# Sixteen hashed-attention heads and two feed-forward blocks on one core: the unit copies of the first two head pairs moved to ScalarE, a third raw buffer, and the product of two weights moved six steps ahead

## The chip, the cores and the metric

The kernel runs on one core of one Trainium2 chip. TensorE multiplies and transposes, ScalarE and VectorE read its results out of PSUM, GpSimd (POOL) and SyncE (SP) issue DMAs. The metric is the device time of one launch in microseconds (us), the median of several runs.

## What is computed

Attention whose mask is "same hash bucket", 2 batches of 8 heads with 768 positions of 64 numbers, then two feed-forward blocks on 1536 tokens of 512 numbers. All is fp32 to the caller; the weights arrive as fp64.

```python
q_bits = (einsum('bhsd,dk->bhsk', q, proj) > 0)       # 6 bits; the same for k
mask = q_bucket[:, :, :, None] == k_bucket[:, :, None, :]
scores = where(mask, scale * q @ k.T, -1e9)
attn = softmax(scores)                                 # row maximum taken off first
x = (attn @ v)  ->  (1536, 512)
h = x @ w_in; g = h * tanh(softplus(h)); x2 = g @ w_out          # d_ff 2048
a = x2 @ w1; b = x2 @ w2; out = ((a * b) @ w3) @ w_out2          # d_ff 1024
```

## The kernel before

**Attention in 96 steps.** A pair of heads is one p (8 pairs). A half of a pair's query rows is one j (16 of them), and a j has 6 steps, each a block of 128 query rows of one head: step n has j = n // 6. `scores` multiplies the block with all keys into a PSUM tile `ts` (two matmuls on `ka`/`qa`, which hold the bits too, two on `kb`/`qb`), `maxima` (VectorE) takes the row maxima, `expo` (ScalarE) takes the exponential into `E`. `unit` transposes three blocks of `E` on TensorE into PSUM (`et`), a copy brings them to SBUF (`etf`), and `av` multiplies them with v. There are 12 unit copies per j, two in each step; before, ScalarE makes 7 of the 12 and VectorE 5. `norm`, `rb_mm`, `rb_act` and `x_out` apply the row sums and store 192 KB of x.

**Preparing a pair.** For each head and each of q and k, `split_hi` (ScalarE) and `split_lo` (VectorE) cut fp32 into two parts, `qk_transpose` transposes them into PSUM (`tqk`), `qk_act` copies that out in two ScalarE activations (`qb`/`kb`, then `qa`/`ka`), `bits_mm` multiplies with the projection (`tb`) and `bits_dve` writes the bits (VectorE, 12x768). The first head is prepared ahead of step 0 (the prologue), the rest inside the steps.

**One ring of two PSUM tiles** (`ps_s`, tag "s") holds `ts`, `tqk`, `tb` and `w3p`. A tile can be written again only when its reader is through: `expo` for `ts`, `qk_act` for `tqk`, `bits_dve` for `tb`.

**Weights.** fp64 arrives as pairs of int32. `load64` (on POOL's queue) loads 1 MB into a raw buffer (2 of them), and three steps turn it into fp32: `decode_a` (ScalarE), `decode_b1` (two VectorE instructions), `decode_b2` (one). Since a*b is followed by two products with no function between, the kernel first computes wp = w3 @ w_out2 in the shadow of attention: w_out2 in four parts (`pre_a` to `pre_c`, `wo2_hi`, `wo2_lo`), w3 in eight blocks of 128 rows (`w3_trans` into `w3p`, `w3_hi`, `w3_lo`), and for each block f 24 matmuls of 512 columns into `wacc` (`wp_mm`), stored by `wp_out`. Later steps decode the first chunks of w_in and w_out (`chunk_dec` to `issue_lo`), split the first x (`x_load`, `x_hi`, `x_lo`) and begin the first feed-forward product (`h_early`, from step 83).

**The order.** `at(n, where, fn)` puts a piece of work at step n; the main loop runs the places of a step in a fixed order, and `pin` keeps every engine to it:

```python
run(n, "pr"); scores; run "la"; maxima; run "nm", "lv", "un", "av", "mm"; expo
then "pe" (transposes, bit products), "ea" (ScalarE), "ev" (VectorE), "dm" (DMAs)
```

So a bit product (`tb`) at a step's "pe" stands behind that step's `ts` and units, and the `bits_dve` of it at the next step's "lv" behind that step's maxima. `MM` says how many of a block's 24 matmuls stand in a step, by n % 6. After attention a list (`prog`) of products over three blocks of 512 tokens runs to the end; its order on each engine is the scheduler's.

Of the kernel before, what the change touches and what calls it, by code (L numbers as in the profile page):

```python
# [18 lines left out]
F32 = mybir.dt.float32  # L19
# [15 lines left out]
def kernel(  # L35
# [43 lines left out]
    def load64(src, n, pool=strm, queue=nc.sync):  # L79
        raw = pool.tile([128, n, 1024 // n, 2], I32, tag="raw", name="raw", bufs=2)  # L80
        queue.dma_start(out=raw.rearrange("p a b t -> p a (b t)"), in_=src)
        return raw, pool
# [393 lines left out]

    def qk_act(u, nm):
        t = spare_ps.pop((u, nm))
        f = [
            pf.tile([128, S], FR, tag=nm + h, name=nm + h, bufs=3) for h in "ab"  # L480
        ]
        feats[u, nm] = f
        scale = 1.0 if nm == "q" else 1.0 / float(D) ** 0.5
        nc.scalar.activation(
            out=f[1].rearrange("p (a n) -> p a n", a=2), in_=t[:, :, 0:HS].bitcast(F32),
            func=AF.Copy, scale=scale,
        )
# [113 lines left out]

    def unit(j, e, kt):
        t = ps.tile([128, 512], F32, tag="et", name="et", bufs=2)
        for ci in range(CH):
            nc.tensor.transpose(  # L605
                t[:, ci * 128:(ci + 1) * 128],
                E[j, e * CH + ci][:, kt * 128:(kt + 1) * 128],
                ident,
            )
        f = pa.tile([128, HS], F32, tag="etf", name="etf", bufs=NR)  # L610
        act = kt % 2 == 0 or (e == 0 and kt == 3)
        (nc.scalar.copy if act else nc.vector.tensor_copy)(out=f, in_=t[:, 0:HS])  # L612
        eth[j, e, kt] = f
# [44 lines left out]
    def pre_c(nm, i):  # L658
        pre[nm, i] = decode_b2(pre[nm, i])
        x = PRE.index((nm, i)) + 2  # L660
        if x < len(PRE):
            pre_load(x)
# [184 lines left out]
    for i, nm in enumerate("qk"):  # L847
# [18 lines left out]
    for n in range(max(NS + 6, HEND + 2)):  # L866
# [188 lines left out]
```

## Time and profile before

| what | value |
|---|---|
| median of 3 runs | 860.73 us (858.62 to 861.25) |
| the profiled execution | 859.71 us, span 857.9 us |
| PE busy | 811.0 us (95%) |
| DVE busy | 513.1 us (60%) |
| ACT busy | 455.7 us (53%) |
| chain that ended last | PE 76%, DVE 12%, ACT 5%, issue 3%, DMA 3% |

The span is the time between the first and the last instruction that the profiler saw; the profiled execution's own time is 1.8 us more. In the table of stretches below, PEclk is the clock that TensorE was granted (1.00 is 2.4 GHz, 0.50 is 1.2 GHz), and the boundaries of the stretches are starts of the maxima instruction (L551) of a step: 12.49 is step 0, 38.66 step 6, 111.23 step 24, 139.07 step 30, 280.36 step 66, 347.41 step 84.

### The profile page before, as it was taken

Reading aid. Unit: us, or ns where it says so; the run is one execution under the profiler, and the core shown is the slowest. Engines: PE = TensorE matmul, PEld = TensorE weight load, DVE = VectorE, ACT = ScalarE, POOL = GpSimd, SP = SyncE. Lnnn points to the kernel's source line nnn. Section 1 sums busy time; section 2 is a strip of 40 time slices with the busy share of each in tenths; the row PEclk is TensorE's granted clock in tenths of the full one; section 3 lists DMA queues with packets and bytes.
Section 4 is the critical chain, followed back from the end, with each engine's and each line's share of the span. In section 5 each row is a group of like instructions: output and inputs, shape, how many; then the busy total and the mean of one; then the engine's idle time right before and its main releaser. Section 6 shows DMA issues by size and latency. Waiting matters only on the chain.

```text
span 857.9 us, 10511 instructions
## 1 busy us (share of the span) xinstructions
PE 811.0 (95%) x4145; PEld 630.0 (73%) x4145; DVE 513.1 (60%) x711; ACT 455.7 (53%) x691; POOL 75.2 (9%) x131
## 2 busy tenths in 40 slices
PE   6678879999999998999999999999999999999998
PEld 4556657777777775677887888888888888888886
DVE  5577777777777788867997874333444343324422
ACT  5566756666667777776654643333343333333321
POOL 1000000000000000101231211000110110110000
PEclk8799989999999999999999999999999999999999
DMA  5112313232322324344887754242332234322101
GB/s 190 56 50 90 131 59 127 70 114 72 126 71 97 123 84 135 126 159 149 300 292 281 247 196 125 96 148 98 107 113 75 82 116 147 98 99 74 48 1 50
DMA packets 34593, 103.45 MB, mean 121 GB/s; under 512 B 3184, under 2 KB 11632, under 8 KB 33520
## 3 DMA queue, kind: packets, MB, share of 16 engines
q0 software_dynamic: 20928, 81.80, 27.9%
q1 hardware_dynamic: 13472, 20.85, 7.2%
q8 instruction: 33, 0.54, 0.3%
q14 instruction: 16, 0.13, 0.0%
q10 hardware_dynamic: 144, 0.13, 0.0%
HBM read 81.79 MB, written 20.97 MB: 120 GB/s over the span
## 4 chain that ended last, share of the span: by engine, by line
PE 76%; DVE 12%; ACT 5%; issue 3%; DMA 3%; POOL 0%; ACTq 0%; DVEq 0%; POOLq 0%
PE abp L944 16%; PE hps L334 12%; PE x2a L917 11%; PE oac L968 8%; PE ts L540 8%; PE pv L620 6%; PE et L605 4%; PE wacc L703 4%; DVE st L551 4%; PE tb L500 3%; DVE qa L509 2%; DMA raw<-in_moe_w_dram 2%; ACT E L562 2%; PE rb L587 2%; PE tqk L470 1%
## 5 line engine op out<-in xcount | busy, mean ns | idle before, releaser
L551 DVE TENSOR_REDUCE st<-ts 128x1 f32<-128x768 f32 x96 | 91.9, 957 | 93.5 <-PE ts L540 93.4
L944 PE MATMUL abp<-x2hl,hl 128*128 128x512 f32 x576 | 137.5, 395 | 0.0
L334 PE MATMUL hps<-xhl,hl 128*128 128x512 f32 x552 | 133.2, 395 | 0.8 <-ACT mh L361 0.8
L917 PE MATMUL x2a<-ghl,hl 128*128 128x512 f32 x552 | 132.0, 397 | 1.7 <-DVE ghl L379 1.7
L944 PEld LDWEIGHTS abp<-x2hl,hl 128*128 128x128 f32 x576 | 108.3, 188 | 25.6
L269 DVE TENSOR_TENSOR hl<-f,hl 128x1024 fp32r<-128x1024 f32 x60 | 73.4, 1224 | 89.7 <-ACT hl L264 89.7
L917 PEld LDWEIGHTS x2a<-ghl,hl 128*128 128x128 f32 x552 | 104.8, 190 | 26.6 <-DVE ghl L379 2.0
L334 PEld LDWEIGHTS hps<-xhl,hl 128*128 128x128 f32 x552 | 102.9, 188 | 26.3 <-issue 2.4
L562 ACT ACTIVATE E<-ts,st 128x768 f32<-128x768 f32 x96 | 95.5, 995 | 26.1 <-DVE st L554 25.7
L612 ACT COPY etf<-et 128x384 f32<-128x384 f32 x112 | 52.1, 480 | 61.4 <-PE et L605 61.1
L605 PE MATMUL et<-ident,E 128*128 128x128 f32 x576 | 82.3, 280 | 0.1
L264 ACT CAST hl<-f 128x1024 fp32r<-128x1024 f32 x60 | 62.8, 1046 | 26.2 <-PE abp L944 12.0
L605 PEld LDWEIGHTS et<-ident,E 128*128 128x128 f32 x576 | 71.1, 144 | 5.6 <-DVE etf L612 0.8
L620 PE MATMUL pv<-etf,rv 128*64 128x384 f32 x384 | 74.3, 510 | 0.0
L540 PE MATMUL ts<-ka,qa 76*128 76x384 f32 x192 | 56.1, 374 | 15.2 <-ACT E L562 9.2
L968 PE MATMUL oac<-hl,phl 128*128 128x512 f32 x288 | 69.8, 393 | 0.0
L968 PEld LDWEIGHTS oac<-hl,phl 128*128 128x128 f32 x288 | 54.2, 188 | 12.4
L953 DVE TENSOR_TENSOR asb<-abp,asb 128x512 f32<-128x512 f32 x24 | 16.6, 691 | 72.2 <-ACT asb L952 72.2
L952 ACT COPY asb<-abp 128x512 f32<-128x512 f32 x24 | 14.0, 585 | 85.0 <-PE abp L944 85.0
L703 PE MATMUL wacc<-wo,w3t 128*128 128x512 f32 x192 | 56.9, 418 | 0.0
L89 ACT ACTIVATE g<-raw 128x1024 f32<-128x1024 f32 x36 | 41.2, 1144 | 27.5 <-DMA raw<-in_moe_w_out_dram 10.4
L379 DVE TENSOR_TENSOR ghl<-mh,ghl 128x1024 fp32r<-128x1024 f32 x24 | 29.3, 1223 | 38.9 <-ACT ghl L378 38.9
(108 smaller groups left out, 967.9 us busy)
## 6 DMA issues: line engine op xcount, KB each, us to landing
raw<-in_moe_w_dram POOLq DMA_DIRECT2D x16, 1024.0 KB, 5.5
raw<-in_moe_w_out_dram POOLq DMA_DIRECT2D x12, 1024.0 KB, 8.1
raw<-in_moe_w_in_dram POOLq DMA_DIRECT2D x8, 1024.0 KB, 6.8
f<-keep_wi POOLq DMA_DIRECT2D x16, 512.0 KB, 3.6
f<-keep_wo POOLq DMA_DIRECT2D x16, 512.0 KB, 3.6
f<-wp_d POOLq DMA_DIRECT2D x12, 512.0 KB, 4.0
keep_wi<-g POOLq DMA_DIRECT2D x8, 512.0 KB, 4.8
keep_wo<-g POOLq DMA_DIRECT2D x8, 512.0 KB, 3.1
```

What stands on the lines that cost most here:

```text
L264: nc.scalar.copy(out=hl[:, 0], in_=f)
L269: nc.vector.tensor_sub(out=hl[:, 1], in0=f, in1=hl[:, 0])
L334: nc.tensor.matmul(o, lhsT=w[:, ws, kk, f * 128:(f + 1) * 128], rhs=xh[xs][:, kk, :], start=(m == 0), stop=(m == 3 * KD - 1),)
L540: nc.tensor.matmul(t[:, a, 0:HS], lhsT=l[0:kk, qt * 128:(qt + 1) * 128], rhs=r[0:kk, a * HS:(a + 1) * HS], start=(l is qa), stop=(l is qb),)
L551: nc.vector.tensor_reduce(out=s[:, i, 1:2], in_=sc[j, i][:, :, 0:HS], axis=AX.XY, op=ALU.max, negate=True)
L562: nc.scalar.activation(out=e.rearrange("p (a n) -> p a n", a=2), in_=sc.pop((j, i))[:, :, 0:HS], func=AF.Exp, scale=s[:, i, 2:3], bias=s[: ...
L605: nc.tensor.transpose(t[:, ci * 128:(ci + 1) * 128], E[j, e * CH + ci][:, kt * 128:(kt + 1) * 128], ident,)
L620: nc.tensor.matmul(pv[j][e * D:(e + 1) * D, 0:HS], lhsT=raws[p, "v"][:, e, kt, :], rhs=eth.pop((j, e, kt)), start=(kt == 0), stop=(kt == C ...
L703: nc.tensor.matmul(wacc[f], lhsT=w3t[f][:, ws, g, :], rhs=wo2[rs][:, g, :], start=(n == 0), stop=(n == 3 * GT - 1),)
L917: nc.tensor.matmul(x2a[n][d], lhsT=w[:, ws, f, d * 128:(d + 1) * 128], rhs=g[:, gs, f, :], start=(j == 0 and f == 0 and s == 0), stop=(j = ...
L944: nc.tensor.matmul(t[:, i, :], lhsT=ws_[i][:, ws, kk, (f % 2) * 128:(f % 2) * 128 + 128], rhs=xh[:, xs, kk, :], start=(m == 0), stop=(m == ...
L968: nc.tensor.matmul(oac[n][t], lhsT=g[:, gs, t * 128:(t + 1) * 128], rhs=w[:, ws, f % 2, :], start=(f == 0 and s == 0), stop=(f == FF2 // 1 ...
```

## The change

It alters tables and three helpers, and no arithmetic.

- In the steps below 24 (`LIGHT`) ScalarE makes all unit copies; from 24 on they are shared out as before.
- In the prologue the second copy of `qk_act` for the first head (`qa`, `ka`) goes to VectorE.
- `bits_dve(1, "k")` of step 2 stands ahead of that step's maxima ("pr") instead of behind them ("lv"). The second pair's first head is prepared a step later, its second head's splits a step later.
- raw buffers in the pool `strm` become three; `pre_load` runs three decodes ahead instead of two, and three loads instead of two are issued at step 0.
- The decoding of w_out2 and of w3's first two blocks is relaid over steps 4 to 23. Blocks f of w3 begin at step 18 + 6f instead of 24 + 6f, and a block's 24 matmuls stand in three steps (n % 6 = 5, 0, 1: 8, 7, 9) instead of six (4, 9, 2, 2, 1, 6 by n % 6).
- The chunks of w_in and w_out and the first x are decoded about 6 steps earlier; `h_early` stays at step 83.

```diff
-        raw = pool.tile([128, n, 1024 // n, 2], I32, tag="raw", name="raw", bufs=2)
+        raw = pool.tile([128, n, 1024 // n, 2], I32, tag="raw", name="raw", bufs=3 if pool is strm else 2)
...
-    def qk_act(u, nm):
+    def qk_act(u, nm, op=None):
...
+        if op:
+            nc.vector.tensor_scalar(
+                out=f[0][0:D].rearrange("p (a n) -> p a n", a=2),
+                in0=half[:, :, 0:HS].bitcast(F32), scalar1=scale, scalar2=None, op0=ALU.mult,
+            )
+            return
...
-    def unit(j, e, kt):
+    def unit(j, e, kt, act):
...
-        act = kt % 2 == 0 or (e == 0 and kt == 3)
...
-    at(2, "lv", lambda: bits_dve(1, "k"))
+    at(2, "pr", lambda: bits_dve(1, "k"))
...
-            if p == 1 and e == 0:
-                nh, nl, nt, nb = 1, 2, nt + 1, nb + 1
+            if p == 1:
+                nh, nl, nt, nb = (5, 6, nt, nb) if e else (2, 3, nt + 2, nb + 2)
...
+    LIGHT = 24
...
-                at(s + 4 + m, "un", lambda j=j, kt=kt: unit(j, 0, kt))
-                at(s + 7 + m, "un", lambda j=j, kt=kt: unit(j, 1, kt))
+                at(s + 4 + m, "un", lambda j=j, kt=kt, n=s + 4 + m: unit(j, 0, kt, n < LIGHT or kt % 2 == 0 or kt == 3))
+                at(s + 7 + m, "un", lambda j=j, kt=kt, n=s + 7 + m: unit(j, 1, kt, n < LIGHT or kt % 2 == 0))
...
-    for i, na, nb, nc_, nh, nl in ((0, 4, 7, 8, 8, 9), (1, 5, 10, 13, 13, 14), (2, 12, 15, 16, 17, 19), (3, 20, 22, 25, 25, 28)):
+    for i, na, nb, nc_, nh, nl in ((0, 4, 5, 7, 8, 9), (1, 5, 8, 9, 10, 10), (2, 10, 13, 14, 15, 18), (3, 19, 20, 21, 22, 22)):
...
-    MM = (4, 9, 2, 2, 1, 6)
+    MM = (7, 9, 0, 0, 0, 8)
...
-        n = 24 + 6 * f
-        na, nb, nc_ = (n - 6, n - 4, n - 3) if f else (17, 20, 21)
+        n = 18 + 6 * f
+        na, nb, nc_ = ((11, 15, 16), (20, 21, 23))[f] if f < 2 else (n - 6, n - 4, n - 3)
...
-    for i, na, nb, nc_, nh, nl in ((0, 66, 68, 69, 70, 73), (1, 70, 74, 75, 76, 79), (2, 76, 80, 81, 82, 85), (3, 81, 82, 86, 87, 88)):
+    for i, na, nb, nc_, nh, nl in ((0, 60, 62, 63, 64, 67), (1, 64, 68, 69, 70, 73), (2, 70, 74, 75, 76, 79), (3, 75, 80, 81, 82, 85)):
...
-        qk_act(0, nm)
+        qk_act(0, nm, True)
```

In the order of instructions three places show it. The first is VectorE in the prologue, from the projection's parts (`psel`) to the first maxima (`st`). Before:

```order
L420 COPY psel<-pq 128x2x6 x4
L455 CAST hlq<-rq 128x6x64
L461 TENSOR_TENSOR hlq<-rq,hlq 128x6x64
L509 TENSOR_SCALAR qa<-tb,ccol 12x768
L509 TENSOR_SCALAR ka<-tb,ccol 12x768
L551 TENSOR_REDUCE st<-ts 128x1
```

and now:

```order
L420 COPY psel<-pq 128x2x6 x4
L490 TENSOR_SCALAR qa<-tqk 64x768
L455 CAST hlq<-rq 128x6x64
L461 TENSOR_TENSOR hlq<-rq,hlq 128x6x64
L490 TENSOR_SCALAR ka<-tqk 64x768
L515 TENSOR_SCALAR qa<-tb,ccol 12x768
L515 TENSOR_SCALAR ka<-tb,ccol 12x768
L557 TENSOR_REDUCE st<-ts 128x1
```

Two copies of 64x768 stand ahead of the two bit instructions, and the first scores need all four.

The second is ScalarE from the exponential of step 8 to that of step 10 (`hl` is a split, `wo` the upper part of w_out2, `etf` a unit copy, `E` an exponential). Before:

```order
L562 ACTIVATE E,st<-ts,st 128x768
L455 CAST hlq<-rq 128x6x64
L455 CAST hlk<-rk 128x6x64
L484 ACTIVATE qb<-tqk 128x768
L489 ACTIVATE qa<-tqk 64x768
L612 COPY etf<-et 128x384
L562 ACTIVATE E,st<-ts,st 128x768
L665 CAST wo_0_108<-g 128x1024
L484 ACTIVATE kb<-tqk 128x768
L489 ACTIVATE ka<-tqk 64x768
L612 COPY etf<-et 128x384
L562 ACTIVATE E,st<-ts,st 128x768
```

and now:

```order
L455 CAST hlq<-rq 128x6x64
L455 CAST hlk<-rk 128x6x64
L670 CAST wo_0_108<-g 128x1024
L484 ACTIVATE qb<-tqk 128x768
L495 ACTIVATE qa<-tqk 64x768
L617 COPY etf<-et 128x384 x2
L568 ACTIVATE E,st<-ts,st 128x768
L484 ACTIVATE kb<-tqk 128x768
L495 ACTIVATE ka<-tqk 64x768
L617 COPY etf<-et 128x384 x2
L568 ACTIVATE E,st<-ts,st 128x768
```

The cast of w_out2 moved a step ahead, and each exponential has two unit copies ahead of it instead of one.

The third is TensorE at steps 23 and 24 (`tb` is a bit product, `rb` the row sums, `w3p` a transposed block of w3). Before:

```order
L540 MATMUL ts<-kb,qb 128x384 x2
L605 MATMUL et<-ident,E 128x128 x6
L500 MATMUL tb<-kb,psel 76x384 x4
L540 MATMUL ts<-ka,qa 128x384 x2
L540 MATMUL ts<-kb,qb 128x384 x2
L605 MATMUL et<-ident,E 128x128 x6
L587 MATMUL rb<-ident,st 64x128 x6
L678 MATMUL w3p<-ident,g 128x128 x8
```

and now, up to the scores of step 24:

```order
L546 MATMUL ts<-kb,qb 128x384 x2
L611 MATMUL et<-ident,E 128x128 x6
L708 MATMUL wacc<-wo_0_108,w3t 128x512
L708 MATMUL wacc<-wo_1_109,w3t 128x512
L708 MATMUL wacc<-wo_0_108,w3t 128x512 x2
L708 MATMUL wacc<-wo_1_109,w3t 128x512
L708 MATMUL wacc<-wo_0_108,w3t 128x512 x2
L708 MATMUL wacc<-wo_1_109,w3t 128x512
L506 MATMUL tb<-kb,psel 76x384 x4
L546 MATMUL ts<-ka,qa 128x384 x2
L546 MATMUL ts<-kb,qb 128x384 x2
```

Eight matmuls of the first block stand between the units of step 23 and its bit product; before, the first block was not yet transposed there.

## Rows read from the trace of the kernel before

**Rows 1.** Stretches: length; busy PE, PEld, DVE, ACT, POOL (instructions); PEclk; DMA share; GB/s

```profile
0.00:12.49 12.49, 9.78 (x47) 7.31 (x47) 7.84 (x27) 5.84 (x8) 3.43 (x13) 1.00 0.82 286
12.49:38.66 26.17, 15.97 (x68) 12.27 (x69) 11.38 (x19) 16.11 (x28) 0.00 (x0) 0.67 0.19 64
38.66:111.23 72.57, 57.48 (x354) 41.15 (x353) 56.88 (x91) 46.76 (x84) 2.54 (x4) 0.93 0.24 82
111.23:139.07 27.84, 23.66 (x137) 16.82 (x136) 19.61 (x30) 16.47 (x29) 1.07 (x2) 0.88 0.32 111
139.07:280.36 141.29, 138.80 (x890) 104.40 (x889) 102.95 (x168) 96.82 (x174) 3.65 (x6) 1.00 0.27 90
280.36:347.41 67.05, 61.52 (x399) 45.10 (x398) 54.56 (x89) 50.99 (x90) 3.87 (x6) 1.00 0.38 123
391.50:857.90 466.40, 460.47 (x2002) 370.81 (x2000) 227.83 (x236) 188.09 (x223) 56.75 (x94) 1.00 0.39 135
```

**Rows 2.** TensorE's waits, 12.49 to 111.23: total us, times, longest us

```profile
PE tb L500 <- DVE qa L509: 7.6, 3, 3.3
PE ts L540 <- ACT E L562: 7.4, 9, 1.6
PE tb L500 <- DVE ka L509: 2.4, 1, 2.4
```

**Rows 3.** Instruction groups, unit copies, 12 to 400: count, busy us, mean ns

```profile
L612 ACT COPY etf<-et 128x384 f32<-128x384 f32 x112 | 52.1, 480 | 61.4 <-PE et L605 61.1
L612 DVE COPY etf<-et 128x384 f32<-128x384 f32 x80 | 44.2, 553 | 0.7
```

**Rows 4.** Timeline of steps 14 and 15: start us, duration us, [idle before, releaser]

```profile
72.59 0.96 DVE L551 TENSOR_REDUCE st<-ts 128x1 f32<-128x768 f32 x1
...
73.78 0.99 ACT L562 ACTIVATE E<-ts,st 128x768 f32<-128x768 f32 x1 [1.22 <-DVE st L554]
...
74.77 0.50 ACT L455 CAST hlq<-rq 128x384 fp32r<-128x384 f32 x1
...
74.92 0.61 PE L540 MATMUL ts<-ka,qa 76*128 76x384 f32 x2 [0.70 <-ACT E L562]
...
75.58 1.04 ACT L665 CAST wo<-g 128x1024 fp32r<-128x1024 f32 x1
...
75.92 0.96 DVE L551 TENSOR_REDUCE st<-ts 128x1 f32<-128x768 f32 x1 [1.71 <-PE ts L540]
...
76.53 0.81 ACT L484 ACTIVATE qb<-tqk 128x768 fp32r<-128x768 f32 x1
...
77.92 0.47 ACT L612 COPY etf<-et 128x384 f32<-128x384 f32 x1
...
78.28 1.00 ACT L562 ACTIVATE E<-ts,st 128x768 f32<-128x768 f32 x1
```

**Rows 5.** Timeline of step 35, all engines

```profile
158.57 0.96 DVE L551 TENSOR_REDUCE st<-ts 128x1 f32<-128x768 f32 x1 [1.38 <-PE ts L540]
...
158.94 1.62 PE L703 MATMUL wacc<-wo,w3t 128*128 128x512 f32 x6
...
159.76 1.07 DVE L509 TENSOR_SCALAR qa<-tb,ccol 12x768 fp32r<-12x768 f32 x1
...
160.98 0.89 PE L500 MATMUL tb<-kb,psel 128*76 128x384 f32 x4 [0.42 <-DVE qa L509]
...
162.62 0.96 DVE L551 TENSOR_REDUCE st<-ts 128x1 f32<-128x768 f32 x1 [1.20 <-PE ts L540]
```

**Rows 6.** Timeline of VectorE at the end of the prologue

```profile
9.36 1.07 DVE L509 TENSOR_SCALAR qa<-tb,ccol 12x768 fp32r<-12x768 f32 x1
10.36 1.07 DVE L509 TENSOR_SCALAR ka<-tb,ccol 12x768 fp32r<-12x768 f32 x1
```

**Rows 7.** One stretch at the lower clock, columns as in rows 1

```profile
118.25:125.07 6.82, 6.56 (x20) 3.93 (x21) 5.22 (x8) 2.18 (x6) 0.54 (x1) 0.50 0.42 154
```

**Rows 8.** TensorE's waits from 391 to the end, columns as in rows 2

```profile
PE x2a L917 <- DVE ghl L379: 1.7, 1, 1.7
```

More of the change, by code (lines that the diff above doesn't have):

```diff
@@ L659, in pre_c @@
         pre[nm, i] = decode_b2(pre[nm, i])
-        x = PRE.index((nm, i)) + 2
+        x = PRE.index((nm, i)) + 3
         if x < len(PRE):
@@ L751 @@
         if p + 1 < NP:
-            at(n0 + 4, "dm", lambda p=p: load_pair(p + 1, "qk"))
+            at(n0 + (4 if p > 1 else 6), "dm", lambda p=p: load_pair(p + 1, "qk"))
+    LIGHT = 24
     for j in range(NJ):
@@ L767 @@
         at(nc_, "ev", lambda i=i: pre_c("o", i))
-        at(nh if nh > nc_ else nh + 1, "ea", lambda i=i: wo2_hi(i))
-        at(nl if nl > nh + 1 or nh > nc_ else nl + 1, "ev", lambda i=i: wo2_lo(i))
-    MM = (4, 9, 2, 2, 1, 6)
+        at(nh, "ea", lambda i=i: wo2_hi(i))
+        at(nl, "ev", lambda i=i: wo2_lo(i))
+    MM = (7, 9, 0, 0, 0, 8)
     for f in range(GT):
-        n = 24 + 6 * f
-        na, nb, nc_ = (n - 6, n - 4, n - 3) if f else (17, 20, 21)
+        n = 18 + 6 * f
+        na, nb, nc_ = ((11, 15, 16), (20, 21, 23))[f] if f < 2 else (n - 6, n - 4, n - 3)
         at(na, "ea", lambda f=f: pre_a(3, f))
@@ L782 @@
             m1 = m + MM[k_ % 6]
-            at(k_, "mm", lambda f=f, m=m, m1=m1: wp_mm(f, m, m1))
+            if m1 > m:
+                at(k_, "mm", lambda f=f, m=m, m1=m1: wp_mm(f, m, m1))
             m = m1
@@ L786 @@
         at(n + 8, "la", lambda f=f: wp_out(f))
-    at(58, "dm", lambda: load_to(1))
-    at(64, "dm", lambda: load_to(2))
-    for i, na, nb, nc_, nh, nl in ((0, 66, 68, 69, 70, 73), (1, 70, 74, 75, 76, 79), (2, 76, 80, 81, 82, 85), (3, 81, 82, 86, 87, 88)):
+    at(52, "dm", lambda: load_to(1))
+    at(56, "dm", lambda: load_to(2))
+    at(60, "dm", lambda: load_to(3))
+    for i, na, nb, nc_, nh, nl in ((0, 60, 62, 63, 64, 67), (1, 64, 68, 69, 70, 73), (2, 70, 74, 75, 76, 79), (3, 75, 80, 81, 82, 85)):
         at(na, "ea", lambda i=i: chunk_dec(i))
@@ L793 @@
         at(nc_, "ev", lambda i=i: chunk_sign(i))
-        at(nc_, "dm", lambda i=i: load_to(i + 3))
+        at(nc_, "dm", lambda i=i: load_to(i + 4))
         at(nh, "ea", lambda: issue_hi())
         at(nl, "ev", lambda i=i: issue_lo(i))
-    for kk, (nd, nh, nl) in enumerate(((69, 74, 75), (70, 75, 76), (75, 79, 80), (76, 80, 81))):
+    for kk, (nd, nh, nl) in enumerate(((63, 68, 69), (64, 69, 70), (69, 71, 72), (70, 74, 76))):
         at(nd, "dm", lambda kk=kk: x_load(0, kk))
@@ L882 @@
         if n == 0:
-            for x in range(2):
+            for x in range(3):
                 with tc.issue_after(next(
```

## The prediction

> **What bounds the kernel now.** I read the table of stretches first [rows 1]. From 391.50 to the end TensorE is busy 460.47 of 466.40 us, and from step 30 to step 66 138.80 of 141.29: there a change that leaves TensorE's work alone can win the rest at most. The idle time lies earlier: 26.17 - 15.97 = 10.2 us in steps 0 to 5, 72.57 - 57.48 = 15.1 in steps 6 to 23, 4.2 in steps 24 to 29, and then 5.5 in steps 66 to 83. The clock column says that the same early stretches ran at 0.67, 0.93 and 0.88 of full speed, so some of their busy time is matmuls of double length.
>
> The table of waits says for what TensorE stood still up to step 24 [rows 2]: 7.6 and 2.4 us for the bits that VectorE writes, 7.4 us for exponentials. Both come from the ring of two PSUM tiles. The timeline of one step shows the second kind [rows 4]: maxima at 72.59, exponential at 73.78, the next scores at 74.92 when the exponential is through, the next maxima at 75.92, a circle of 3.33 us. It holds wherever another tile (`tqk`, `tb`) was drawn between two scores, that is in steps 2 to 5 of each six. ScalarE can stretch it, since all that stands between two exponentials counts: here 73.78 to 78.28, 4.50 us. The first kind is the step that is 5 of six [rows 5]: maxima at 158.57, bits at 159.76, the bit product at 160.98 only when the bits are written, next maxima at 162.62, a circle of 4.05 us in which TensorE idles 0.42 us even with six matmuls of the weights' product in it.
>
> So three limits make a step, and the largest counts: the circle (3.33, or 4.05), ScalarE's list between exponentials, TensorE's own work. I worked through the steps of the new order with them.
>
> **The change part by part.** All differences stand against the profiled execution, 859.71 us.
>
> *Prologue.* VectorE gets two instructions on 768 columns of PSUM. The trace has none of that form; the bit instruction has the same length and starts every 10.36 - 9.36 = 1.00 us [rows 6], the maxima over 768 last 0.96 [rows 4]. VectorE sets the end of the prologue, since the scores need the second bits at once, and ScalarE, which is relieved, does not. So 2 x 1.00 = **+2.0 us**; if they find gaps, +1.0, and nothing in the order lets them win.
>
> *Steps 0 to 5, 26.17 us before.* The wait of 2.4 us for `ka` [rows 2] was the bits of step 2 behind that step's maxima; now they are ahead: -2.4. The second pair's transposes leave step 3, so the scores of step 4 draw a free tile and follow at VectorE's pace (1.1 of maxima, 1.0 of two splits) instead of the circle at the low clock, 3.33 + 0.7: -1.9. The second unit copy on ScalarE in steps 4 and 5 gives 0.7 back. **-3.6**; between -5 and -1.5, since the low clock may last longer or shorter than before.
>
> *Steps 6 to 23, 72.57 us before.* Each unit copy that changes engine costs ScalarE 0.48 and saves VectorE 0.55 [rows 3]; 17 change in steps 4 to 23. Whether that is worth anything depends on the step. ScalarE's list by starts [rows 4]: two splits 0.81, cast of a weight 0.95, the two copies of q 1.39, exponential 1.0, two unit copies 0.9; `decode_a` (same size) taken as 1.0, the copies of k as 1.5. Step 21 has splits, `decode_a`, q, units and exponential: 5.1. Step 6 has 5.3. Step 9 has 5.1 too, but 0.8 of it falls into a step that VectorE stretches: 4.3. Steps 10, 15, 16, 22: 3.5, 4.2, 4.45, 3.5. Three steps are the 4.05 circle (11, 17, 23), steps 7 and 8 have 4.1 each (bits, then decoding on VectorE), step 18 has 4.15 with the first transposes of w3 in it. The other five (12, 13, 14, 19, 20) run at 3.0 to 3.4, 16.5 together. Sum: 14.7 + 15.65 + 12.15 + 8.2 + 4.15 + 16.5 = 71.35, so **-1.2**. ScalarE takes back most of what VectorE is spared. The bounds are -5 (the lists overlap better) and +3 (bit products at the low clock, which add about 0.7 to a step). The eight matmuls that now stand in step 23 are free: TensorE waited for the bits there.
>
> *Steps 24 to 29, 27.84 us before.* This stretch held the start of the weights' product and 6.82 us at clock 0.50 with TensorE busy 6.56 [rows 7]. In the new order block 0 is transposed at step 18, and from step 24 the stretch is like the six that follow: 141.29 / 6 = 23.55 a time [rows 1], less the 0.42 below. **-4.7**. But idle TensorE time now stands in steps 18 to 22, so a stretch at 0.50 may fall here again, or on one of the three circles of 4.05 before it; such a stretch in full work costs half of 6.6, 3.3. I add **+1.5** for that, and keep 0 and +4 for the range.
>
> *Steps 30 to 65, 141.29 before.* The step of rows 5 gets 8 matmuls instead of 6: by 1.62 / 6 the two take 0.5, more than the idle 0.42. Steps 2 to 4 of each six lose theirs; the scores of step 3 then come 0.5 earlier, and the circle of 3.33 stays under TensorE's own 3.5 or so. 6 x 0.42 = **-2.5**, the whole idle of that stretch in rows 1; 0 if the thinner steps begin to wait.
>
> *Steps 66 to 83, 67.05 before.* Here the filling is gone six steps earlier. Steps 68 to 72 lose their matmuls, but fall on the circles and on ScalarE's lists (splits, x, copies of q: 4.2 at step 69): some 1.2 less than before. Against it, steps 80 to 82 get the decoding of two chunks on VectorE, 1.2 to 1.6 more than before. **-0.1**, between -2 and +3.
>
> *From step 84 on.* Less decoding lies beside the first `h_early` products; they were busy all the time but 0.8 us: **-0.5**. In the feed-forward blocks TensorE waited once, 1.7 us for `ghl` [rows 8]. The third raw buffer lets POOL's loads run further ahead, and VectorE's order of decoding and `ghl` is another. The work is the same: **0**, between -3.4 (that wait and the low clock behind it gone) and +4 (two such waits). SP's loads of pairs move by two steps and nobody waited for them.
>
> Sum: 2.0 - 3.6 - 1.2 - 4.7 + 1.5 - 2.5 - 0.1 - 0.5 = -9.1, so 850.6 for an execution like the profiled one. That one lay 1.0 under the median of 860.73, so **851.6** in the metric.
>
> **The rivals.**
> 1. *ScalarE becomes the bound, slower.* If every moved copy lengthens its step from step 4 to 23, 17 x 0.48 = 8.2 us stand in place of the -1.2 and of the -1.9 of steps 4 and 5, and if the thinned steps also wait, the -2.5 goes: -9.1 + 8.2 + 1.2 + 1.9 + 2.5 = +4.7, 865.4. It decides where ScalarE's list exceeds the circle of 3.33 in most steps. Against it: ten of those twenty steps have lists under 3.
> 2. *The idle only moves to the end.* Steps 67 to 82 have no filling now, and idle TensorE time there can bring the low clock: before, steps 66 to 83 idled 5.5 us and the clock stayed at 1.00 [rows 1], which speaks against it. A stretch of 6.8 us at 0.50, and the same again at a bit product or a wait in the feed-forward blocks, cost 4 together: 855.6. By the Trainium skill (TensorE: Matmul & The Clock Gate, section Why this matters for your kernels) idle stretches between bursts of matmuls are what takes the clock down; by that rule this rival is likelier than the trace makes it, at the same price.
> 3. *The wait of rows 8 goes.* With loads further ahead -1.7, and 1.7 of low clock behind it: 848.2.
> 4. *Nothing to measure.* The dense start at step 24 gets its low clock back (+3.2 beyond the 1.5) and the gains of steps 0 to 23 are eaten by ScalarE's lists (+4.8): 859.6.
>
> **How the numbers follow.** Forecast (849 to 854) 0.50, rival 2 0.18, rival 3 0.15, rival 4 0.10, rival 1 0.07. Faster by over 0.3% means under 858.1, about what a measurement of this kernel can tell from no change: the forecast and rivals 2 and 3, 0.83; the same 0.10; slower 0.07. The range leaves out rival 1, most of rival 4 and the far end of rival 3: 846 to 858.
>
> **What would show it.** Right: the first maxima at 14.4 instead of 12.49, step 6 at 37, step 24 near 108, steps 30 to 65 in 139 us with no wait of TensorE for bits in them, and step 84 some 8 to 9 us earlier. Wrong: a clock under 1.00 between steps 24 and 30, waits of TensorE for exponentials in steps 30 to 65, steps 66 to 83 over 69 us, or new waits for `ghl`.

## Result and profile after

The changed kernel takes **848.84 us** (median of 4 runs, 847.05 to 849.40), the kernel before 860.74 in the same comparison: ratio **0.9863, 95% interval 0.9841 to 0.9885**, faster by 10 to 14 us. The profiled execution took 849.40 us, span 847.6.

Stretches of the changed kernel, cut at the same steps as rows 1 (step 0, 6, 24, 30, 66, 84 and the last maxima), columns as there:

```profile
0.00:14.31 14.31, 10.60 (x47) 8.04 (x47) 9.66 (x28) 4.43 (x6) 4.14 (x14) 1.00 0.85 298
14.31:36.11 21.80, 15.66 (x64) 12.43 (x65) 11.57 (x19) 14.61 (x27) 0.00 (x0) 0.65 0.15 58
36.11:111.20 75.09, 60.01 (x374) 43.49 (x373) 55.74 (x82) 56.92 (x105) 2.89 (x5) 0.94 0.31 104
111.20:134.17 22.97, 22.97 (x150) 17.49 (x149) 17.16 (x29) 16.35 (x29) 1.06 (x2) 1.00 0.41 146
134.17:272.32 138.15, 138.15 (x890) 105.08 (x889) 102.96 (x169) 99.99 (x176) 4.60 (x7) 1.00 0.29 97
272.32:339.03 66.71, 56.49 (x370) 40.64 (x369) 55.17 (x89) 48.55 (x87) 5.17 (x8) 1.00 0.38 124
379.96:847.63 467.67, 462.61 (x2022) 372.39 (x2020) 229.99 (x242) 190.87 (x228) 56.09 (x93) 1.00 0.39 133
```

From step 24 to step 66 TensorE is busy without a gap. But step 24 starts at 111.20, where it stood at 111.23 before: of the 4.4 us that the first six steps won the prologue takes 1.8 and steps 6 to 23 take 2.5. The last line answers to 388.26 to 857.94 of before, 469.68 us.

What TensorE waited for in the first 24 steps, and in the last line what it waited for after attention (us in total, times, longest), against rows 2 and 8:

```profile
PE ts L546 <- ACT E L568: 9.5, 11, 1.7
PE tb L506 <- DVE qa L515: 6.8, 4, 2.6
PE rb L593 <- DVE st L583: 1.4, 2, 0.9
...
PE x2a L925 <- DVE ghl L379: 0.5, 1, 0.5
```

The wait for `ka` of rows 2 is gone and the wait for `ghl` is down from 1.7 to 0.5; the waits for exponentials grew from 7.4 to 9.5.

| part | predicted | profiled execution |
|---|---|---|
| prologue | +2.0 | +1.8 |
| steps 0 to 5 | -3.6 | -4.4 |
| steps 6 to 23 | -1.2 | **+2.5** |
| steps 24 to 29 | -4.7 + 1.5 | -4.9 |
| steps 30 to 65 | -2.5 | -3.1 |
| steps 66 to 83 | -0.1 | -0.3 |
| step 84 to the last maxima | -0.5 | +0.1 |
| behind them | 0 | **-2.0** |
| sum | -9.1 | -10.3 |

### The profile page after: what moved, and what is told of

Its sections match the earlier page's. It is cut to its first block, busy times and chain, and to the rows that moved or that the text cites. A ratio compares the mean times of both kernels' runs of the same rounds, so it can differ in the third digit from the quotient of the medians.

```text
span 847.6 us, 10509 instructions
## 1 busy us (share of the span) xinstructions
PE 806.5 (95%) x4145; PEld 628.9 (74%) x4145; DVE 506.3 (60%) x697; ACT 461.3 (54%) x705; POOL 75.2 (9%) x131
## 4 chain that ended last, share of the span: by engine, by line
PE 74%; DVE 10%; ACT 8%; issue 4%; DMA 3%; POOL 0%; SPq 0%; DVEq 0%; ACTq 0%; POOLq 0%
PE abp L952 16%; PE hps L334 12%; PE x2a L925 10%; PE oac L976 8%; PE ts L546 7%; PE pv L625 5%; PE wacc L708 5%; PE et L611 5%; PE tb L506 3%; DVE st L557 3%; ACT E L568 2%; PE rb L593 1%; ACT etf L617 1%; DMA raw<-in_moe_w_in_dram 1%; DVE qa L515 1%
## 5 line engine op out<-in xcount | busy, mean ns | idle before, releaser
L925 PE MATMUL x2a<-ghl,hl 128*128 128x512 f32 x552 | 130.3, 394 | 0.5 <-DVE ghl L379 0.5
L617 ACT COPY etf<-et 128x384 f32<-128x384 f32 x128 | 58.1, 479 | 54.5 <-PE et L611 54.0
L625 PE MATMUL pv<-etf,rv 128*64 128x384 f32 x384 | 72.3, 498 | 0.0
L960 ACT COPY asb<-abp 128x512 f32<-128x512 f32 x24 | 14.1, 587 | 85.2 <-PE abp L952 85.2
L89 ACT ACTIVATE g<-raw 128x1024 f32<-128x1024 f32 x36 | 41.1, 1145 | 26.4 <-DVE hl L269 12.2
L546 PE MATMUL ts<-kb,qb 128*128 128x384 f32 x192 | 51.2, 349 | 0.0
```

What stands on the lines that cost most here:

```text
L546: nc.tensor.matmul(t[:, a, 0:HS], lhsT=l[0:kk, qt * 128:(qt + 1) * 128], rhs=r[0:kk, a * HS:(a + 1) * HS], start=(l is qa), stop=(l is qb),)
L625: nc.tensor.matmul(pv[j][e * D:(e + 1) * D, 0:HS], lhsT=raws[p, "v"][:, e, kt, :], rhs=eth.pop((j, e, kt)), start=(kt == 0), stop=(kt == C ...
L925: nc.tensor.matmul(x2a[n][d], lhsT=w[:, ws, f, d * 128:(d + 1) * 128], rhs=g[:, gs, f, :], start=(j == 0 and f == 0 and s == 0), stop=(j = ...
```

## Experiments

All ratios are to the kernel before, run beside them (860.4 to 861.3 us). "Back" means undone in the changed kernel, "alone" added to the kernel before.

| kernel | median us | ratio | 95% interval |
|---|---|---|---|
| changed kernel | 848.84 | 0.9863 | 0.9841 to 0.9885 |
| prologue back | 847.96 | 0.9856 | 0.9836 to 0.9876 |
| copies back | 850.65 | 0.9894 | 0.9871 to 0.9918 |
| even spread back | 853.57 | 0.9923 | 0.9904 to 0.9941 |
| two raw buffers | 853.50 | 0.9908 | 0.9890 to 0.9926 |
| start at step 24 | 850.59 | 0.9895 | 0.9867 to 0.9924 |
| third raw buffer alone | 858.76 | 0.9977 | 0.9958 to 0.9997 |
| first six steps alone | 855.19 | 0.9942 | 0.9921 to 0.9962 |
| copies alone | 858.89 | 0.9982 | 0.9967 to 0.9997 |
| picked copies | 846.96 | 0.9857 | 0.9829 to 0.9885 |
| picked, filled | 843.19 | 0.9808 | 0.9786 to 0.9831 |
| **picked, filled better** | **842.00** | **0.9780** | 0.9753 to 0.9807 |
| filling alone | 856.73 | 0.9947 | 0.9924 to 0.9969 |

### The prologue

```diff
-        qk_act(0, nm, True)
+        qk_act(0, nm)
```

> The changed kernel, but the first head's second copies (qa, ka) go back to ScalarE in the prologue. In the traces the first maxima started at 12.49 before and at 14.31 after. Theory: a late start is carried to the end, since each step waits for the one before; the first maxima start near 12.5 and the time is 848.8 - 1.8 = 847.0. Rival: the later steps wait for something else (loads of the raw buffers, or a stretch at the lower clock that then falls differently), so that the 1.8 us are gone by step 24 and the time stays at 848.8.

Measured: 847.96 us. Neither figure stands out: the intervals of the two kernels overlap almost wholly. The first maxima start at 13.05 here. Over the profiles of all kernels with the copies on ScalarE (this, the kernel before, and seven below) the start lies between 12.17 and 13.05, mean 12.7; with the copies on VectorE (the changed kernel and four below) between 13.37 and 14.50, mean 14.1. So the two instructions cost about 1.4 us, and the start itself wanders by 0.9 to 1.1. Step 24 starts at 111.46 in this profile, later than the 111.20 of the changed kernel although step 0 starts 1.3 earlier: steps 6 and 18, on which stretches at 0.50 lay, took 7.01 and 4.98 instead of 5.99 and 4.16. That is what the rival said, in one profile.

### The copies

```diff
-    LIGHT = 24
+    LIGHT = 0
```

> The changed kernel with LIGHT = 0: the unit copies are shared between ScalarE and VectorE as before in all steps, all else as in the changed kernel. Steps 6 to 23 took 75.09 us there, 72.57 before. Theory: the moved copies lengthen ScalarE's list between two exponentials by 0.48 each and that is why the stretch is longer; it falls to 72.5 to 73.5 and the time to 846.3 to 847.2. Rival: the moved copies relieve VectorE, and the stretch is longer for the relaid decoding or for the lower clock at its end; then it grows to 77 to 78 and the time to 851 to 852.

Measured: 850.65 us, between the two. Steps 6 to 23 took 76.05 at clock 0.91. A stretch at 0.50, from 92.9 to 96.3, fell on step 20 (5.05 instead of 3.52); the other seventeen steps together changed from 71.57 to 71.01, and without steps 6 and 11, where the clock differs too, from 60.48 to 59.62. By that the moved copies cost the stretch 0.6 to 0.9, and where the clock falls costs more. The same copies alone in the kernel before:

```diff
-        act = kt % 2 == 0 or (e == 0 and kt == 3)
+        act = early or kt % 2 == 0 or (e == 0 and kt == 3)
...
-                at(s + 4 + m, "un", lambda j=j, kt=kt: unit(j, 0, kt))
+                at(s + 4 + m, "un", lambda j=j, kt=kt, n=s + 4 + m: unit(j, 0, kt, n < 24))
```

(and likewise for the other head)

> The kernel before with the unit copies of the steps below 24 all on ScalarE, and nothing else. In the changed kernel taking these back cost 1.8 us by the medians, of which its profile shows 1.5 as a stretch at the lower clock in step 20. Theory: a copy more or less hides behind the circle of 3.33 and behind VectorE's list alike; the time is 860.6 within 1, and steps 6 to 23 stay within 1 of 72.6. First rival: ScalarE becomes the bound, 17 copies of 0.48 lengthen their steps, and the time is 865 or more. Second rival: VectorE's relief pays by itself; the time is 859 or less.

Measured: 858.89 us, 0.3 to 2.8 faster by the interval; steps 6 to 23 took 72.09 instead of 72.57, steps 0 to 5, at a clock of 0.56, 27.36 instead of 26.17. So ScalarE did not become the bound. The theory's "within 1" and the rival's "859 or less" both lie in the interval: a small gain, its size left open.

### The bursts

```diff
-    MM = (7, 9, 0, 0, 0, 8)
+    MM = (4, 9, 2, 2, 1, 6)
```

> The changed kernel with the old spread of the 24 matmuls of the weights' product over six steps, MM = (4, 9, 2, 2, 1, 6); the start at step 18 stays. Theory: the bursts win the idle 0.42 us ahead of each bit product from step 30 on, 2.5 to 3.1 us in all; the time is 851.3 to 851.9, and TensorE waits some 0.4 us in every sixth step for VectorE's bits. Rival: the bursts only move the idle time, and the 3.1 us were won by the two-thirds of the shared-out decoding that also moved; the time stays at 848.8.

Measured: 853.57 us, the whole loss the theory wanted and 1.7 more. Steps 30 to 65 of this kernel, and its timeline where `tb` is drawn (start, duration, [idle before, releaser]):

```profile
137.20:278.51 141.31, 138.82 (x890) 104.46 (x889) 102.90 (x168) 98.68 (x176) 4.59 (x7) 1.00 0.29 96
...
157.10 1.62 PE L708 MATMUL wacc<-wo,w3t 128*128 128x512 f32 x6
...
159.14 0.89 PE L506 MATMUL tb<-kb,psel 128*76 128x384 f32 x4 [0.41 <-DVE qa L515]
```

In the changed kernel the same place reads:

```profile
153.51 2.07 PE L708 MATMUL wacc<-wo,w3t 128*128 128x512 f32 x8
...
155.55 0.89 PE L506 MATMUL tb<-kb,psel 128*76 128x384 f32 x4
```

141.31 is the 141.29 of before, with the same 0.41 idle ahead of `tb` in each sixth step; two more matmuls (0.45) fill it. That is 3.2 of the loss and 0.6 more lies in steps 24 to 29. Steps 66 to 83 gain 0.7 by the old spread, since it leaves four instead of seven of the last block's matmuls in step 66 (3.34 instead of 3.96). Step 20, with two of the matmuls in it, fell into a stretch at 0.50 (5.16 instead of 3.52); whether the spread brought that stretch there is not shown.

### Two raw buffers or three

```diff
-        raw = ... bufs=3 if pool is strm else 2)
+        raw = ... bufs=2)
```

> The changed kernel with two raw buffers in place of three; the loads are still issued as far ahead, so a load waits for its buffer on its queue. After attention TensorE's wait for ghl was 1.7 us before and 0.5 in the changed kernel, and the stretch from step 95 on 469.6 and 467.6. Theory: the third buffer brought that; the wait is back at about 1.7 with 1.7 of lower clock behind it, and the time is 850.8. Rival: the order of decoding alone brought it, or the earlier decoding; the time stays at 848.8. If a load that waits for its buffer holds up the decoding before step 24, steps 6 to 23 grow over 75.1 and the time over 851.

Measured: 853.50 us, a loss of 4.7 where 2 was expected; steps 6 to 23 did not grow (74.80). Its last stretch, and TensorE's waits in it:

```profile
380.45:852.25 471.80, 464.68 (x2022) 373.35 (x2020) 230.73 (x242) 191.47 (x228) 56.32 (x94) 1.00 0.40 134
...
PE x2a L925 <- DVE ghl L379: 1.7, 1, 1.7
PE abp L952 <- ACT mh L347: 0.8, 1, 0.8
PE x2a L925 <- ACT ghl L378: 0.5, 1, 0.5
```

The third buffer alone, in the kernel before:

```diff
-        raw = ... bufs=2)
+        raw = ... bufs=3 if pool is strm else 2)
```

> The kernel before with a third raw buffer alone; the loads of w_out2 and w3 are issued as far ahead as before. With two buffers in the changed kernel the stretch after attention took 471.8 us instead of 467.7 and TensorE waited 1.7 us for ghl, 0.8 and 0.5 elsewhere. Theory: the third buffer is worth that by itself; the wait of 1.7 us for ghl and the lower clock behind it go, the stretch of 469.7 becomes 466.4 to 467.7 and the time 857.4 to 858.7. Rival: it pays only with the earlier decoding; the time stays at 860.8.

Measured: 858.76 us, at the theory's upper end; its profile had a last stretch of 466.42 instead of 469.68, with 0.2 us of waits in all. Over all profiles of this study the last stretch takes 469.5 to 471.8 in the five kernels with two buffers and 466.4 to 469.0 in the nine with three, 3.1 less by the means. The two timelines say how. The kernel before, ahead of the wait of rows 8:

```profile
462.73 0.76 POOL L81 DMA_DIRECT2D raw<-in_moe_w_dram  x1
...
464.26 1.13 ACT L89 ACTIVATE g<-raw 128x1024 f32<-128x1024 f32 x1 [1.29 <-DMA raw<-in_moe_w_dram]
465.30 1.03 ACT L378 CAST ghl<-mh 128x1024 fp32r<-128x1024 f32 x1
...
467.31 1.22 DVE L379 TENSOR_TENSOR ghl<-mh,ghl 128x1024 fp32r<-128x1024 f32 x1
...
468.58 6.70 PE L917 MATMUL x2a<-ghl,hl 128*128 128x512 f32 x21 [1.69 <-DVE ghl L379]
```

and with the third buffer:

```profile
454.81 17.89 PE L917 MATMUL x2a<-ghl,hl 128*128 128x512 f32 x77
...
457.06 1.12 ACT L89 ACTIVATE g<-raw 128x1024 f32<-128x1024 f32 x1 [2.67 <-DVE hl L269]
...
461.67 1.05 ACT L378 CAST ghl<-mh 128x1024 fp32r<-128x1024 f32 x1 [1.60 <-PE x2a L917]
...
463.50 1.22 DVE L379 TENSOR_TENSOR ghl<-mh,ghl 128x1024 fp32r<-128x1024 f32 x1
```

With two buffers ScalarE stood 1.29 us at the decoding, for a load that was issued only when the chunk ahead was merged, and the cast of `ghl` stood behind it in ScalarE's order; VectorE and TensorE inherit the delay. With three the data is there and TensorE works through. The prediction named the wait and the order of VectorE, but not this chain.

### The first six steps alone

```diff
-    at(2, "lv", lambda: bits_dve(1, "k"))
+    at(2, "pr", lambda: bits_dve(1, "k"))
...
-            if p == 1 and e == 0:
-                nh, nl, nt, nb = 1, 2, nt + 1, nb + 1
+            if p == 1:
+                nh, nl, nt, nb = (5, 6, nt, nb) if e else (2, 3, nt + 2, nb + 2)
```

(with the load of the next pair two steps later, as in the change; the second head's splits go from steps 2 and 4 to steps 5 and 6, which is more than the one step that the section on the change says)

> The kernel before with the relaid preparation of steps 1 to 6 alone: the bits of step 2 ahead of that step's maxima, the second pair prepared a step later. The copies, the raw buffers, the decoding and the weights' product stay as they were. Steps 0 to 5 took 26.17 us before and 21.80 in the changed kernel, and step 24 began at 111.23 and 111.20. Theory: the gain of 4.4 is carried on, step 24 begins near 106.9 and the time is 856.4; then the relaid decoding lost it in the changed kernel. Rival: the steps behind it give it back by themselves, since the stretches at the lower clock fall on fuller steps; step 24 begins near 110 or later and the time is 859.5 to 860.8.

Measured: 855.19 us, the theory's time and 1.2 below it. In its profile step 24 starts at 109.19, between the two. Steps 0 to 5, 6 to 23 and 24 to 29 are

```profile
12.87:34.65 21.78, 14.73 (x64) 11.82 (x65) 10.18 (x17) 13.16 (x25) 0.00 (x0) 0.68 0.09 35
34.65:109.19 74.54, 59.18 (x358) 42.55 (x357) 57.72 (x92) 48.94 (x87) 2.53 (x4) 0.91 0.27 90
109.19:135.53 26.34, 22.16 (x137) 16.33 (x136) 19.60 (x31) 16.46 (x29) 1.07 (x2) 0.94 0.35 119
```

4.4 are won in the first six steps, 2.0 are lost in the next eighteen, where step 6 takes 6.94 instead of 5.05 at the lower clock; the relaid decoding has no part in that.

### The start of the product

```diff
-        n = 18 + 6 * f
-        na, nb, nc_ = ((11, 15, 16), (20, 21, 23))[f] if f < 2 else (n - 6, n - 4, n - 3)
+        n = 24 + 6 * f
+        na, nb, nc_ = (n - 6, n - 4, n - 3) if f else (17, 20, 21)
```

(with the tables of w_out2, of the chunks and of x as before; the bursts stay)

> The changed kernel with the product's start back at step 24 and all tables of decoding back to those of before; the bursts of 7 to 9, the copies in the first 24 steps, the three raw buffers and the first six steps stay as changed. Theory: the early start won 4.9 us in steps 24 to 29 and cost 2.5 in steps 6 to 23 through its relaid decoding; steps 6 to 23 fall to 72 or 73, steps 24 to 29 grow to 27 or 28, and the time is 851.2. Rival: steps 6 to 23 are longer because of the unit copies or the clock, not the decoding; they stay near 75 and the time is 853.7 or more.

Measured: 850.59 us, the theory's figure, but not in the theory's stretches: steps 6 to 23 stay at 73.96, and steps 24 to 29 take 25.51. By these rows the early start won 2.5 there and cost 1.1 ahead of it. The clock hides a part of that cost, for here a stretch at 0.50, from 86.1 to 92.9, lies on steps 18 and 19, and in the changed kernel none does. The steps that the clock touched in neither profile (7 to 10, 13 to 17, 20 to 23) are 1.1 longer with the early start; steps 18 and 19 take 7.50 in the changed kernel and 6.00 in the kernel with the third buffer alone, both at full clock. So at equal clock the early start and its relaid decoding cost some 2.6 by this estimate, about the theory's 2.5. Of the 4.9 in steps 24 to 29 the missing 2.3 were never its own. In the five profiles with the kernel before's spread and its start at 24, steps 24 to 29 took 27.84 and 27.80 at a mean clock of 0.88, and 26.34, 26.38 and 26.40 at 0.94: rows 7 was the dearer of two kinds. The Trainium skill (TensorE: Matmul & The Clock Gate, section What's actually happening) says that the unit which sets the clock does not start anew with a kernel, so that one kernel's slow matmuls differ in number between runs. The five profiles are in line with that; they are of five kernels that differ ahead of step 24, so they do not show it.

### A picked version

```diff
-    LIGHT = 24
+    LIGHT = (4, 5, 6, 7, 8, 11, 13, 14, 17, 18, 19, 20, 23)
...
-... n < LIGHT or ...
+... n in LIGHT or ...
...
-        qk_act(0, nm, True)
+        qk_act(0, nm)
```

> A version made from the two looks at the unit copies and the one at the prologue: the changed kernel with the first head's second copies on ScalarE, and with all unit copies on ScalarE only in the steps below 24 where this step was shorter so (or as short) in the traces with and without it; in steps 9, 10, 12, 15, 16, 21 and 22 they are shared as before. The seven steps were 0.72, 0.05, 0.2, 0.38, 0.36, 0.31 and 0.06 us shorter with shared copies: 2.1 in all, and the prologue gave 0.9. Theory: steps add up as long as the clock's stretches stay; the time is 845.8 to 846.7. Rival: copies that stay on VectorE in one step delay the next step as much, or a stretch at the lower clock falls on a full step; the time is 848 to 850.

Measured: 846.96 us, a little above the theory's range, and not told apart from the changed kernel. Steps 15, 16 and 21 did as expected (3.56, 3.95, 4.58, where the changed kernel has 3.94, 4.32, 4.94), step 9 gave half (4.17, where 4.53 less 0.72 was expected) and step 12 nothing (3.76 and 3.70): the seven steps gave 1.5 of the 2.1. Step 20 fell into a stretch at 0.50 (5.05) and step 6 into another (6.97). Most profiles so far had won or lost 1 to 2 us that way, so the clock itself was tried.

### Filling

Added to the picked version (`warm` multiplies zeros, `m` matmuls into one PSUM tile):

```diff
+    for n, m in ((0, 6), (1, 6), (2, 6), (4, 4), (5, 3), (17, 4), (19, 4)):
+        at(n, "dm", lambda m=m: warm(m))
```

> The picked version with filling on TensorE: 33 matmuls of 512 columns whose result nobody reads, behind the transposes or the bit product of steps 0, 1, 2, 4, 5, 17 and 19 (6, 6, 6, 4, 3, 4, 4), where TensorE stood idle for 1 to 1.8 us. In the picked version the clock was 0.50 in three stretches within steps 0 to 11 and in one around step 20; steps 1 and 2 took 4.07 and 4.09, step 6 took 6.97, step 20 took 5.05, where the same steps took 3.3 to 3.5, 5.05 (before) and 3.52 at full clock. Theory: the longer first steps are the clock, and the clock falls because of the idle; with filling it stays at 1.00, steps 1, 2, 6 and 20 shorten by 0.7, 0.7, 1.9 and 1.5, and the time is 842 to 843.5. Rival: the lower clock follows from something else, or the filling itself stands ahead of the scores; the stretches at 0.50 stay and the time is 847 to 852.

Measured: 843.19 us, as the theory has it. The first six steps and the next eighteen:

```profile
12.17:31.83 19.66, 16.29 (x89) 12.76 (x90) 11.56 (x18) 13.85 (x27) 0.00 (x0) 1.00 0.27 106
31.83:105.46 73.63, 59.39 (x382) 43.25 (x381) 59.02 (x89) 55.08 (x98) 2.88 (x5) 0.98 0.31 106
```

Steps 1, 2 and 6 take 3.43, 3.32 and 5.24. One stretch at 0.50 is left, in step 7, and step 17 is 0.93 longer, since its filling stands ahead of the scores:

```profile
78.78 0.89 PE L506 MATMUL tb<-kb,psel 128*76 128x384 f32 x4 [1.79 <-DVE qa L515]
...
79.51 1.10 PE L830 MATMUL warm<-zr 128*128 128x512 f32 x4
...
80.44 0.52 PE L546 MATMUL ts<-ka,qa 76*128 76x384 f32 x2
```

Both mended, still on the picked version (`warm` now takes the tile's tag and number of buffers; this line of the helper is left out here):

```diff
+    for where, tag, bufs, steps in (
+        ("dm", "p", None, ((0, 6), (1, 6), (2, 6), (4, 4), (5, 3), (19, 4))),
+        ("mm", "p", None, ((6, 5), (7, 5))), ("mm", "et", 2, ((11, 5), (17, 5)))):
+        for n, m in steps:
+            at(n, where, lambda m=m, tag=tag, bufs=bufs: warm(m, tag, bufs))
```

> The filled version with its filling better placed. In the first one the filling of step 17 stood behind the bit product and ahead of the scores, waited for the x that VectorE reads out, and made the step 4.98 instead of 4.05; step 7 still ran at clock 0.50 (5.26 instead of 4.04). Here the filling of step 17 stands ahead of the bit product, and five matmuls each are added in steps 6, 7 and 11 at that place, where TensorE waited 1.74, 1.79 and 2.40 us. Theory: the 0.93 of step 17 and the 1.2 of step 7 go and the clock is 1.00 throughout; 843.2 - 2.1 = 841.1. Rival: the filling's own tiles hold up the transposes of the units, and the steps 6, 7, 11 and 17 lengthen by what is filled; 843 to 845.

Measured: **842.00 us, ratio 0.9780**, the fastest kernel of this study, faster than the changed one by some 7 us. Steps 0 to 5, 6 to 23, and 66 to 83:

```profile
12.67:32.36 19.69, 16.24 (x89) 12.75 (x90) 11.56 (x19) 13.92 (x27) 0.00 (x0) 1.00 0.25 97
32.36:103.56 71.20, 62.15 (x398) 44.53 (x397) 59.04 (x88) 55.19 (x98) 2.89 (x5) 1.00 0.31 109
...
264.66:332.15 67.49, 57.90 (x370) 41.84 (x369) 55.20 (x89) 48.56 (x87) 5.17 (x8) 0.97 0.37 124
```

The time lies between the theory's 841.1 and the rival's 843. Steps 7 and 17 are back at 3.98, 2.3 less together; but the clock was not 1.00 throughout, since a stretch at 0.50 fell on steps 77 and 78 and cost 0.8. The filling alone, in the kernel before (the line of the helper left out here too):

```diff
+        ("dm", "p", None, ((0, 6), (1, 6), (2, 6), (4, 4), (5, 3))),
+        ("mm", "p", None, ((6, 5), (7, 5))), ("mm", "et", 2, ((11, 5), (17, 5)))):
```

> The kernel before with the same filling in steps 0, 1, 2, 4, 5, 6, 7, 11 and 17, and nothing else. Theory: the lower clock lengthened steps 1 to 6 and 10 to 11 there too, by 0.7 each where the circle was stretched; the stretches at 0.50 within steps 0 to 12 go and the time is 857 to 858.5, so that most of what the changed kernel won in its first six steps was the bits' place and not the clock. Rival: the first steps' long waits were the clock's doing; then the time falls below 856. If the filling only takes the place of idle time, it stays at 860.6.

Measured: 856.73 us, just below the theory's range. Steps 0 to 5 and 6 to 23, and TensorE in step 2:

```profile
12.60:37.81 25.21, 19.64 (x93) 16.07 (x94) 11.38 (x19) 16.17 (x28) 0.00 (x0) 0.86 0.20 69
37.81:107.83 70.02, 58.32 (x374) 41.11 (x373) 56.85 (x91) 46.69 (x84) 2.54 (x4) 1.00 0.25 85
...
21.93 0.99 PE L500 MATMUL tb<-qb,psel 128*76 128x384 f32 x4 [2.44 <-DVE ka L509]
22.71 2.77 PE L822 MATMUL warm<-zr 128*128 128x512 f32 x6
25.27 0.84 PE L540 MATMUL ts<-ka,qa 76*128 76x384 f32 x2
```

At full clock steps 6 to 23 of the kernel before take 70.02. Steps 0 to 5 stay at 25.21, of which step 2 still takes 6.99 (6.85 before). Its wait of 2.44 for `ka` is the 2.4 of rows 2, though the clock stood at 1.00 until 22.6: this wait is the order's, as the prediction had it. Behind it the clock fell all the same, and the filling, six matmuls in 2.77 us, stood ahead of the scores; so what step 2 would take at full clock is not shown.

## Why the prediction was right, and where it was not

The time, 848.84, lies inside the range, 2.8 below the forecast and nearer to rival 3's 848.2. Of the signs, the first maxima (14.31), step 6 (36.11), steps 30 to 65 (138.15, no waits) and step 84 (8.4 earlier) came as said, and step 24, "near 108", did not (111.20). Point by point:

- **Prologue, +2.0.** Right in kind, too high: about 1.4 over all profiles.
- **Steps 0 to 5, -3.6.** Right. The wait for `ka` went and step 3 fell to 2.02; alone in the kernel before the part is worth 5.4 us by the medians (95%: 3.3 to 6.8).
- **Steps 6 to 23, -1.2: the step that failed.** It measured +2.5. Two things were wrong. First, steps 10 and 22 were given 3.5 from ScalarE's list. In these two steps the new order has both halves of a part of w_out2, the cast on ScalarE (`wo2_hi`) and the subtraction on VectorE (`wo2_lo`), and the next maxima stand behind the subtraction. Step 22 of the changed kernel:

```profile
103.95 1.01 ACT L568 ACTIVATE E<-ts,st 128x768 f32<-128x768 f32 x1
...
104.93 1.05 ACT L670 CAST wo<-g 128x1024 fp32r<-128x1024 f32 x1
...
105.83 0.52 PE L546 MATMUL ts<-kb,qb 128*128 128x384 f32 x2
...
106.01 1.23 DVE L673 TENSOR_TENSOR wo<-g,wo 128x1024 fp32r<-128x1024 f32 x1 [1.21 <-ACT wo L670]
...
107.16 0.95 DVE L557 TENSOR_REDUCE st<-ts 128x1 f32<-128x768 f32 x1
```

  The scores are written at 106.35, but the maxima start at 107.16: exponential, cast and subtraction follow one another over two engines and make the step 4.44. Step 10 has the same chain and takes 4.43; together that is 1.9 more than predicted. In the kernel with the copies alone, step 22 has TensorE's same work and the same unit copies but no half of w_out2, and takes 3.88. The prediction's three limits counted each engine for itself, and a chain through two of them was none of the three.

  Second, the list was made at full clock and set against 72.57, a row at clock 0.93. At full clock the kernel before takes 70.02, so the list's 71.35 stood for a loss of 1.3. The changed kernel's own stretch had 0.94. In step 11 one sees it:

```profile
59.39 0.95 DVE L557 TENSOR_REDUCE st<-ts 128x1 f32<-128x768 f32 x1
...
61.79 1.38 PE L506 MATMUL tb<-kb,psel 128*76 128x384 f32 x4 [2.56 <-DVE qa L515]
...
62.97 0.84 PE L546 MATMUL ts<-ka,qa 76*128 76x384 f32 x2
...
64.49 0.96 DVE L557 TENSOR_REDUCE st<-ts 128x1 f32<-128x768 f32 x1 [2.26 <-PE ts L546]
```

  Behind a wait of 2.56 the bit product takes 1.38 instead of 0.9 and the scores 0.84 instead of 0.5: a step of 5.10, which is 3.98 in the better filled version. Steps 6, 11 and 12 are longer than there by 0.75, 1.12 and 0.30. So -1.2 + 1.9 + 2.2 = +2.9, and the other steps come to -0.4 together: for these the list held. The clock took about as much from either kernel, 2.2 here and 72.57 - 70.02 = 2.6 before. Without it the changed kernel would take 75.1 - 2.2 = 72.9, an estimate, against 70.02, so this part of the change is a loss of some 2.9; the picked version, with 71.20, loses 1.2. Against the kernel before at full clock, steps 8, 9, 16, 18 and 19 are longer by 0.7 to 1.0 each and steps 7, 10 and 15 shorter by 0.6 to 1.0. A slip of counting changed little: 16 copies move in steps 4 to 23 (ScalarE makes 24 of the 40 before, 40 now), not 17.
- **Steps 24 to 29, -4.7 + 1.5.** -4.9, and the reserve was not needed: the clock stood at 1.00 in these steps in every profile with the early start and the bursts (22.96 to 22.98). Against the usual 26.4 of the old order the gain is 3.4; the rest was the dear kind of rows 7.
- **Steps 30 to 65, -2.5.** -3.1, right in cause: the one idle gap per six steps was filled, and the even spread brought it back. The steps that lost their matmuls did not begin to wait.
- **Steps 66 to 83, -0.1.** -0.3. TensorE idled 10.2 us there (66.71 - 56.49), almost twice as long as before, and the clock stayed at 1.00. Rival 2 did not come about, but it exists: the picked and the better filled version each had one stretch at 0.50 around step 77, for 0.9 and 0.8 us. The rule of the Trainium skill that the prediction set beside it (TensorE: Matmul & The Clock Gate, section Why this matters for your kernels), that idle between bursts takes the clock down, goes the same way as the first 24 steps and the filled versions, and mostly not as these. Even in the first 24 steps no idle of TensorE in the changed kernel was longer than 2.6 us, and the page speaks of longer ones.
- **Behind attention, 0.** -2.0: rival 3, to which 0.15 was given. Its price, 3.4, is about what the third buffer alone gave in the profile (466.42 instead of 469.68, 3.3); the changed kernel won 2.0 of it in its one profile, and gave up 4.1 without the buffer.
- **Rival 1** is refuted by the copies alone: no loss. **Rival 4** did not occur, though a half of it did: the gains of the first steps were eaten by step 24, by the prologue (1.8) and by steps 6 to 23 (2.5). ScalarE's lists have a part in it (steps 9, 15, 16 and 21 were 0.3 to 0.7 shorter with shared copies), the chain of steps 10 and 22 has another.

The forecast was thus right in its sum partly because two misses offset each other: +3.7 in steps 6 to 23 against -2.0 behind attention and 1.5 of reserve. The parts don't add up either: first steps 5.4, bursts 4.7, buffer 1.9 to 4.7, start 1.8 and copies 1.5 to 1.8 make over 15, less the prologue's 1.4, against 11.9. The profiles show one reason, the stretches at 0.50 that fall elsewhere in nearly every version; that it is the only one was not shown.

## What to carry to other kernels

List every engine for every step, and the chains that pass from one engine to the next within it: a cast on ScalarE, its subtraction on VectorE and what stands behind that are longer together than the list of either. Set a list made at full clock against a row at full clock: where the granted clock is below 1.00, ask first which idle time brings it down, and whether matmuls that nobody reads can fill that idle for nothing. They must stand ahead of what TensorE waits for, not behind it. A buffer more for loads is worth a look wherever a decoding waits for DMA and the engine that waits has something on the critical path queued behind it.

## What the runs showed of the hardware

- In the first 24 steps of the changed kernel TensorE stood still for up to 2.6 us at a time, and the clock fell to 1.2 GHz in three stretches. With matmuls in that idle, in the picked version, it stayed at 2.4 GHz but for one stretch in step 7, and with the filling placed better in all 24 steps (mean granted clock of steps 0 to 5 0.65 in the changed kernel, and 1.00 in both filled versions, for 0.6 us more of busy time). In the kernel before the same filling left two stretches at 1.2 GHz in steps 0 to 5 (mean 0.86). Steps 66 to 83 idled 10.2 us and mostly kept 2.4 GHz.
- Where a stretch at 0.50 falls is not settled by the step it falls on: kernels with the same instructions in step 6 took 5.91 to 7.02 there, and in step 20 3.52 and 5.05. What settles it was not shown. A difference of 1 to 2 us between two versions, read from one profile of each, may be nothing else.
- The first maxima wander by 0.9 us between kernels with the same instructions in the prologue (12.17 to 13.05).
